# A recurrent attention layer and two feed-forward layers on one core: a new hand-written order for the first 1100 steps

## The chip, the cores and the metric

The kernel runs on one core of a Trainium2 chip. The metric is the device time of one execution in microseconds (us), from runs on the chip. The profile and the trace are of one execution, whose span runs from the first to the last instruction of the core.

## What is computed

Three layers follow one another. The first is a gated recurrent attention with 4 batches, 8 heads, 768 positions and a head dimension of 40. The second and third are feed-forward layers on 3072 tokens of 320 features with 2048 hidden features, both in float32.

```python
for t in range(S):
    m_new = np.maximum(f_gate[:, :, t] + m, i_gate[:, :, t])
    f_stab = np.exp(f_gate[:, :, t] + m - m_new)
    i_stab = np.exp(i_gate[:, :, t] - m_new)
    C = f_stab * C + i_stab * outer(vt, kt)
    n = f_stab * n + i_stab * kt
    y[:, :, t] = sigmoid(o_gate) * (C @ qt) / np.maximum(np.abs(n @ qt), 1.0)
x = y as (3072, 320)
h = x @ w_in;  x = (h * np.clip(h + 3, 0, 6) / 6) @ w_out
h = x @ w2_in; x = np.maximum(h, 0) ** 2 @ w2_out
```

## The kernel before

**Attention.** The recurrence is cut into chunks of 64 positions. A unit is one batch and one chunk; there are 48 units, and a unit of a batch needs the state that the unit before it in the same batch left. The first eight units are (batch 0, 1; chunk 0), (batch 0, 1; chunk 1), then the same for batches 2 and 3. For a unit u the steps are: loads (`at_qk`, `at_kn`, `at_va`), decay weights (`at_rg`, L349, and `w_pe`, L371 and L373, and `w_e`, L393, for the first 16 units; `at_gload`, `w_add`, `w_mask`, `w_e` with L380, L386 and L404 later), scores `at_S` (L450 to L465), their product with the weights `at_P` (L474 to L481), weighted keys `x_k` (L422, L425), output and new state `at_Y` (L492), copy of the state `at_C` (L500), and the normalisation `at_n1` (L508 to L512), `at_n2` (L522 on ACT, L525 on DVE), `at_n3` (L535), which multiplies the output gate in tile X by the result. The gates come first: `gate_m`, `gate_g`, `gate_G`, `gate_b`, `gate_bT` (L277 to L324), in part 0 for the first four chunks and part 1 for the rest. `o_sig` (L542) applies the sigmoid to the output gate of two chunks.

**Feed-forward.** Two chunks of all four batches make a token block of 512 columns. `t_pe` (L639) transposes one batch of it on PE, `t_hi` (L652) and `t_lo` (L668, L670) split the result into two tiles xs. A slot s is one block times 128 hidden features: `mm_A` (8 matmuls, L683), `act1` (ACT, L692), `act1b` (DVE, L701), `act2` (the rounded copy gh, ACT or DVE, L709), `act2b` (the rest gl, DVE, L714), and per batch `mm_B` (3 matmuls, L724). The slots 0 to 7 and 8 to 15 hold half a block each, 0 to 7 of batches 0 and 1, and 8 to 15 of batches 2 and 3; from slot 16 on a slot is a whole block. Weights arrive as 64-bit words (`w_load`, L565) and are unpacked by `w_exp` (ACT, L577), `w_b1` and `w_b2` (DVE, L583 and L589), `w_hi` (L598) and `w_lo` (L603, POOL or DVE). Weight 2i is the i-th eighth of w_in and weight 2i+1 that of w_out.

**What sets the order.** Each engine runs its instructions in the order in which the program issues them, and all loads and stores go through one queue, SP's. The table FIRST (L32 to L119) lists steps with their arguments and, behind an @, the engine where it isn't the usual one (a is ACT, v is DVE, g is POOL). All steps of FIRST are issued in that order, and then those of a planned sequence that FIRST doesn't hold:

```python
todo = [(steps[name], *args) for each entry of FIRST]
early = set(todo)
todo += [step for step in seq if step not in early]
for f, *a in todo:
    f(*a)
```

Of the kernel before, what the change touches and what calls it, by code (L numbers as in the profile page):

```python
# [38 lines left out]
at_Y:1 at_rg:4 w_load:0,3 at_C:0@v at_n1:0 w_load:0,10 at_n2:0@a w_load:0,9 w_pe:4 at_rg:5@v
at_kn:4 at_n1:1 at_n3:0@g at_S:2 at_n2:1 at_C:1@v x_k:2 at_va:6 w_hi:0,0 at_n3:1@g w_exp:0,1 w_pe:5  # L40
at_P:2,0 w_e:4 at_rg:6 at_S:3 w_load:0,4 at_qk:5 w_lo:0,0@v w_exp:0,7 w_b1:0,1 at_Y:2 w_e:5
w_b2:0,1 w_exp:0,2 at_qk:6 at_P:3,0 x_k:3 w_pe:6 w_hi:0,1 at_n1:2 at_rg:7 at_n2:2@a at_S:4
w_load:0,8 w_b1:0,2 w_b2:0,2 at_C:2 w_pe:7 w_exp:0,3 at_rg:8@v at_kn:5 at_P:4,0 at_n3:2@g w_hi:0,2
at_Y:3 w_e:7 w_lo:0,2 w_e:6 t_pe:0,0,0 at_n1:3 at_kn:6 w_exp:0,9 at_C:3@v w_load:0,6 t_hi:0,0,0
at_n2:3@a at_va:7 at_n3:3 t_lo:0,0,0 x_k:4 t_pe:0,0,1 w_lo:0,1 w_exp:0,10 at_Y:4 t_hi:0,0,1@v
at_va:8 t_lo:0,0,1 w_exp:0,4 at_va:9 w_b1:0,3 at_qk:7 mm_A:0 at_C:4 w_b1:0,4 at_n1:4 w_b2:0,4
mm_A:1 act1:0 at_kn:7 at_n2:4 w_hi:0,4 at_va:10 act1b:0 at_S:5 at_n3:4@g act2:0@v at_qk:8 act1:1
act2b:0 w_exp:0,8 w_lo:0,4 act1b:1 mm_A:2 at_P:5,0 act2:1 mm_B:0,1 act2b:1 act1:2 w_load:0,11
at_S:6 w_exp:0,6 w_b2:0,3 at_qk:9 mm_A:3 x_k:5@v w_hi:0,3 act1b:2 x_k:6 at_kn:8 at_Y:5 at_P:6,0
act2:2 w_load:0,5 w_lo:0,3 act1:3 mm_B:0,0 at_va:11 act2b:2 at_C:5 at_S:7 act1b:3 at_va:12 at_n1:5  # L50
act2:3 at_n2:5 x_k:7 at_qk:10 mm_A:4 at_P:7,0 at_kn:9 at_Y:6 w_exp:0,11 w_b1:0,6 load_gates:1
w_b2:0,6 w_pe:8 act1:4 mm_B:1,0 at_C:6 mm_B:2,0 act2b:3 at_rg:9 w_e:8 mm_B:1,1 act1b:4 w_hi:0,6
mm_B:2,1 at_n1:6 w_pe:9 at_rg:10 at_n2:6 act2:4 mm_B:3,1 w_exp:0,5 act2b:4 mm_B:3,0 at_n3:6 w_e:9
mm_A:5 w_b1:0,5 w_lo:0,6@v at_Y:7 act1:5 o_load:3 w_b2:0,5 at_S:8 x_k:8@a at_qk:11 at_n1:7 mm_A:6
at_P:8,0 o_load:2 at_C:7 act1b:5 w_pe:10 at_rg:11 w_hi:0,5 w_load:0,13 w_b1:0,8 o_load:1 at_n3:5
act2:5 act1:6 w_load:0,12 act2b:5 w_lo:0,5 w_e:10 act1b:6 mm_A:7 at_va:13 act2:6@v o_sig:3
w_load:0,14 at_n2:7@a t_pe:0,0,2 act2b:6 at_n3:7@g at_kn:10 mm_B:4,1 t_hi:0,0,2@v mm_B:5,1 at_kn:11
t_lo:0,0,2 mm_B:4,0 mm_B:5,0 w_b1:0,7 t_pe:0,0,3 w_b2:0,7 at_va:14 gate_m:1 act1:7 at_Y:8 w_hi:0,7
act1b:7 at_va:15 t_hi:0,0,3 w_lo:0,7 at_n1:8 act2:7 at_n2:8@a t_lo:0,0,3 act2b:7 mm_A:8 gate_g:1
at_va:16 o_sig:1 mm_B:6,1 mm_B:7,1 at_C:8 act1:8 mm_A:9 w_b2:0,8 gate_G:1 w_exp:0,13 w_exp:0,12  # L60
mm_B:6,0 w_hi:0,8 mm_B:7,0 act1b:8 at_n3:8@g at_S:9 act1:9 act2:8@v act2b:8 o_sig:2 w_lo:0,8
act1b:9 mm_A:10 at_qk:12 act2:9@v w_exp:0,14 act2b:9 mm_B:8,2 at_P:9,0 mm_B:8,3 act1:10 mm_A:11
w_b1:0,12 act1b:10 mm_B:9,2 w_b1:0,9 act2:10 w_pe:11 act1:11 act2b:10 at_rg:12 mm_B:9,3 act1b:11
w_e:11 mm_A:12 gate_b:1 mm_B:10,2 mm_B:10,3 act2:11 x_k:9@v at_kn:12 at_S:10 act1:12 w_b2:0,12
o_load:5 at_Y:9 act2b:11 x_k:10 w_hi:0,12 at_kn:13 at_P:10,0 mm_A:13 at_C:9 w_lo:0,12 act1b:12
at_va:17 mm_B:11,3 at_n1:9 act2:12 mm_B:11,2 at_n2:9 at_qk:13 act1:13 at_S:11 act1b:13 at_n3:9@g
act2b:12 act2:13 at_Y:10 act2b:13 at_va:18 w_b2:0,9 mm_A:14 at_C:10 gate_bT:1 w_hi:0,9 at_qk:14
mm_A:15 act1:14 x_k:11@v o_load:4 mm_B:12,2 act1b:14 w_lo:0,9 act1:15 at_kn:14 mm_B:12,3 at_P:11,0
act2:14 mm_B:13,3 mm_B:13,2 act2b:14 w_pe:12 w_b1:0,10 mm_A:16 act1b:15 at_rg:13 w_e:12 at_n1:10
act2:15 at_n2:10@a act2b:15 w_b1:0,14 at_S:12 w_b2:0,14 act1:16 mm_A:17 at_qk:15 w_b2:0,10  # L70
w_hi:0,14 act1b:16 w_lo:0,14 mm_B:14,2 at_P:12,0 act1:17 mm_B:15,2 act2:16@v mm_B:14,3 w_pe:13
act1b:17 at_rg:14 mm_B:15,3 w_e:13 act2b:16 at_Y:11 act2:17 w_hi:0,10@v w_pe:14 at_va:19 at_C:11@v
at_rg:15 mm_B:16,3 w_e:14 mm_B:16,1 at_n1:11 mm_B:16,2 at_n2:11@a w_lo:0,10 act2b:17 w_load:0,15
at_S:13 mm_B:17,3 at_P:13,0 at_qk:16 mm_B:16,0 mm_B:17,0 w_b1:0,11 w_pe:15 w_b2:0,11 mm_A:18 w_e:15
at_n3:11 w_hi:0,11 x_k:12@v w_exp:0,15 x_k:13@v at_gload:16 mm_B:17,2 at_n3:10 at_kn:15 act1:18
at_Y:12 w_b1:0,15 at_va:20 mm_A:19 act1b:18 w_lo:0,11 at_C:12 at_n1:12 at_kn:16 at_n2:12@a
at_gload:17 act2:18@v w_add:16 at_S:14 act2b:18 w_b2:0,15 mm_B:18,3 act1:19 at_qk:17 at_Y:13
w_b1:0,13 w_hi:0,15 mm_A:20 w_b2:0,13 at_va:21 at_C:13 x_k:14@a at_n1:13 w_add:17 at_n2:13 act1b:19
mm_B:17,1 w_mask:16 mm_B:18,1 at_P:14,0 act2:19 mm_B:18,0 at_kn:17 w_mask:17 mm_B:18,2 at_gload:18
w_e:16 act2b:19 at_S:15 act1:20 at_n3:12 at_n3:13 w_hi:0,13 mm_B:19,3 at_qk:18 mm_B:19,0 at_P:15,0  # L80
x_k:15@a w_lo:0,13 mm_B:19,2 act1b:20 at_S:16 at_Y:14 w_lo:0,15@v act2:20 mm_A:21 at_kn:18 at_va:22
at_n1:14 w_add:18 w_e:17 act2b:20 at_gload:19 at_C:14 at_n2:14 w_mask:18 mm_A:22 act1:21 x_q:16
at_P:16,1 at_P:16,0 w_e:18 act1b:21 t_pe:0,1,0 act2:21 x_k:16@v mm_B:20,0 at_qk:19 mm_B:20,2
t_hi:0,1,0@v at_n3:14@g act1:22 at_gload:20 at_Y:15 t_lo:0,1,0 at_va:23 mm_B:20,3 w_add:19 act2b:21
at_C:15 t_pe:0,1,2 mm_B:19,1 at_n1:15 at_kn:19 mm_A:23 w_mask:19 at_n2:15@a act1b:22 x_q:17
act2:22@v t_hi:0,1,2@v mm_B:21,0 w_e:19 t_lo:0,1,2 w_add:20 mm_B:20,1 act1:23 mm_B:21,3 act2b:22
# [829 lines left out]
```

## Time and profile before

| what | us |
|---|---|
| median of 3 runs (826.83 to 830.62) | 827.2 |
| the profiled execution | 827.76 |
| its span | 826.0 |
| PE busy | 801.1 (97%) |
| DVE busy | 541.9 (66%) |
| ACT busy | 424.8 (51%) |
| POOL busy | 226.8 (27%) |

PE is TensorE, DVE is VectorE, ACT is ScalarE, POOL is GpSimd and SP is the engine that issues the transfers. The shares are means over the whole span. On the page's view in 40 slices PE is busy for nine tenths or more in all slices but the first two, the fourth and the last, and its granted clock is below full in the second and, less, in the fourth.

### The profile page before, as it was taken

The numbers are of one execution on the slowest core, as the hardware profiler recorded it, in microseconds if no ns is written. First come the engines' busy times: TensorE is split into PE (matmuls) and PEld (weight loads), VectorE is DVE, ScalarE is ACT, GpSimd is POOL, SyncE is SP. The second block draws the span as 40 slices with busy tenths as digits, with TensorE's granted clock in tenths as the row PEclk, the third lists the DMA queues.
The fourth block names the chain that finished last, engine by engine and source line by source line (L and its number), as shares of the span: only waits on it lengthen the run. The fifth ranks groups of instructions, "written<-read, shape, count | busy, mean of one in ns | idle before, by whom it ended". The sixth has DMA issues, their size and how long they took to land.

```text
span 826.0 us, 19222 instructions
## 1 busy us (share of the span) xinstructions
PE 801.1 (97%) x7896; PEld 712.3 (86%) x7896; DVE 541.9 (66%) x967; ACT 424.8 (51%) x839; POOL 226.8 (27%) x201
## 2 busy tenths in 40 slices
...
GB/s 230 295 187 182 119 124 72 128 92 72 145 103 108 86 148 99 90 148 36 53 55 235 203 172 1 1 71 1 34 37 1 71 2 1 33 1 0 33 2 33
DMA packets 39332, 72.26 MB, mean 87 GB/s; under 512 B 5420, under 2 KB 25452, under 8 KB 39244
## 3 DMA queue, kind: packets, MB, share of 16 engines
...
q14 instruction: 26, 0.21, 0.1%
...
## 4 chain that ended last, share of the span: by engine, by line
PE 91%; ACT 3%; DVE 3%; issue 2%; POOL 1%; ACTq 0%; DVEq 0%; POOLq 0%
PE hps L683 42%; PE acc L724 40%; PE Yp L492 4%; PE Sp L458 2%; PE tp L639 1%; PE Sp L450 1%; DVE qs L436 1%; PE Sp L452 1%; ACT yt L522 1%; PE Sp L465 0%; PE Wp L373 0%; ACT X L542 0%; DVE X L731 0%; ACT L542 0%; ACT g L692 0%
## 5 line engine op out<-in xcount | busy, mean ns | idle before, releaser
L683 PE MATMUL hps<-xs,wi 128*128 128x512 f32 (+1 forms) x1600 | 389.6, 386 | 1.5 <-DVE gl L714 1.0
L724 PE MATMUL acc<-wo,gh 128*128 128x320 f32 x1536 | 346.2, 312 | 0.0
L683 PEld LDWEIGHTS hps<-xs,wi 128*128 128x128 f32 x1600 | 287.5, 190 | 51.4 <-DVE gl L714 1.6
L724 PEld LDWEIGHTS acc<-wo,gh 128*128 128x128 f32 x1536 | 260.9, 188 | 11.8
L724 PE MATMUL acc<-wo,gl 128*128 128x320 f32 x768 | 237.6, 309 | 0.0
L714 DVE TENSOR_TENSOR gl<-g,gh 128x512 fp32r<-128x512 f32 x176 | 130.6, 743 | 63.2 <-ACT gh L709 61.0
L704 DVE TENSOR_TENSOR g<-g 128x512 f32<-128x512 f32 x96 | 66.4, 691 | 124.3 <-ACT g L694 124.3
L724 PEld LDWEIGHTS acc<-wo,gl 128*128 128x128 f32 x768 | 144.4, 188 | 0.2 <-DVE gl L714 0.2
L692 ACT ACTIVATE g<-hps,less 128x512 f32<-128x512 f32 (+1 forms) x104 | 68.1, 656 | 138.2 <-PE hps L683 126.9
L709 ACT CAST gh<-g 128x512 fp32r<-128x512 f32 x169 | 104.4, 619 | 61.8 <-DVE g L704 49.3
L694 ACT ACTIVATE g<-hps 128x512 f32<-128x512 f32 x96 | 57.3, 597 | 144.7 <-PE hps L683 144.7
L701 DVE SCALAR_TENSOR_TENSOR g<-g,hps 128x512 f32<-128x512 f32 x80 | 54.6, 685 | 52.8 <-ACT g L692 52.6
L414 POOL TENSOR_TENSOR Xm<-qkt,W 40x512 f32<-40x512 f32 x31 | 40.8, 1315 | 105.8 <-ACT W L404 81.2
L603 POOL TENSOR_TENSOR wi<-wt,wi 128x768 fp32r<-128x768 f32 x14 | 27.3, 1953 | 106.9 <-ACT wi L598 101.7
L380 POOL TENSOR_TENSOR W<-W,bT 104x512 f32<-104x512 f32 x32 | 44.8, 1401 | 17.5 <-DMA W<-Gd 12.8
L492 PEld LDWEIGHTS Yp<-Z,Xm 104*32 104x32 f32 (+1 forms) x3072 | 34.8, 110 | 14.1 <-issue 10.9
L492 PE MATMUL Yp<-Z,Xm 104*32 104x41 f32 (+1 forms) x3072 | 40.7, 208 | 0.9 <-issue 0.9
L436 DVE SCALAR_TENSOR_TENSOR qs<-qs,less,qkt 120x512 fp32r<-120x512 f32 x52 | 37.9, 769 | 3.3 <-ACT qs L434 3.1
L603 POOL TENSOR_TENSOR wo<-wt,wo 128x640 fp32r<-128x640 f32 x15 | 24.8, 1656 | 27.6 <-ACT wo L598 27.5
L535 DVE TENSOR_TENSOR X<-X,yt 64x320 f32<-64x320 f32 x34 | 30.1, 887 | 3.0 <-ACT yt L522 2.1
L425 POOL TENSOR_TENSOR Xm<-kI,W 104x320 f32<-104x320 f32 x32 | 30.1, 939 | 5.0 <-DVE pre L349 3.1
L450 PEld LDWEIGHTS Sp<-qkt 40*64 40x64 f32 x256 | 19.3, 157 | 13.3 <-issue 6.6
(110 smaller groups left out, 674.4 us busy)
## 6 DMA issues: line engine op xcount, KB each, us to landing
...
```

The lines of the kernel that those rows point to most:

```text
L380: on("w_add", "g", u).tensor_tensor(out=W, in0=W, in1=bT[:, c - NC1, b * H:(b + 1) * H].unsqueeze(2).to_broadcast([KX, H, L]), op=ALU.add)
L436: nc.vector.scalar_tensor_tensor(out=y[0:KS, i], in0=y[0:KS, i].bitcast(F32), scalar=less[0:KS, i:i + 1], in1=x[0:KS, i], op0=ALU.mult, op ...
L492: nc.tensor.matmul(out=Yp[o:e, h, :], lhsT=Xm[:, h, o:e], rhs=Z[b][c % 2][:, h, :], start=True, stop=True)
L603: on("w_lo", "g", ph, i).tensor_tensor(out=w[:, 1], in0=f, in1=w[:, 0].bitcast(F32), op=ALU.subtract)
L683: nc.tensor.matmul(out=h, lhsT=w[:, hl, kk, o:o + P], rhs=t[:, xk, i0 * P:i1 * P], start=(i == 0), stop=(i == len(TERMS) - 1))
L692: nc.scalar.activation(out=g, in_=T["h", s], func=ACTF.Relu, bias=three)
L694: nc.scalar.activation(out=g, in_=T["h", s], func=ACTF.Relu)
L701: nc.vector.scalar_tensor_tensor(out=g, in0=r, scalar=6.0, in1=T["h", s], op0=ALU.min, op1=ALU.mult)
L704: nc.vector.tensor_tensor(out=g, in0=r, in1=r, op=ALU.mult)
L709: copy("act2", s)(out=gh, in_=g)
L714: nc.vector.tensor_tensor(out=gl, in0=g, in1=gh.bitcast(F32), op=ALU.subtract)
L724: nc.tensor.matmul(out=acc[i], lhsT=g[:, n], rhs=w[:, hl, m % MG, :], start=(m == 0 and q == 0), stop=(m == NM - 1 and q == 2))
```

## The change

The table FIRST is replaced: it held 898 steps and now holds 1100. The engine marked behind an @ is the same for every step. The 202 steps that come in were in the planned sequence that follows the table; 32 of them issue no instruction (`x_q` for the first 16 units, and the second half of `at_P` for these and from unit 22 on). The table now reaches to `act2b:48` and `mm_B:46`, where it reached to `act2b:39` and `mm_B:37`. No function is changed; the lines behind the table move down by 19, so L393 here is L412 there.

```diff
 FIRST = """
-const_z:2 const_i load_gates:0 const_z:3 head_rows:3@g const_m head_rows:2 const_l const_o
...
-x_k:26@a at_P:25,0 act2b:39
+x_q:14 const_i const_z:3 const_o load_gates:0 head_rows:2 const_k:2 at_qk:1 const_z:0 at_va:0
+w_load:0,0 const_m x_q:13 head_rows:3@g head_rows:1 const_g gate_m:0 gate_g:0 gate_G:0 at_qk:0
...
+at_n3:29 mm_B:46,3 at_P:7,1 at_P:24,1 mm_B:46,2
 """
```

Three places show what moves. The first is ACT ahead of slot 0. In the rows W<-Wp is `w_e`, rwi or rwo is `w_exp`, Z<-Yp is `at_C`, yt is `at_n2`, xs is `t_hi:0,0,0`, wi and wo are `w_hi`. Before:

```order
L522 ACTIVATE yt_483<-Yp_432,rd_478 64x40 x8
L500 COPY Z00_101<-Yp_432 40x328
L577 ACTIVATE rwo1_342<-rwo1_342 128x640
L598 CAST wi1_525<-wt_512 128x768
L393 ACTIVATE W_516<-Wp_517 104x512
L393 ACTIVATE W_472<-Wp_473 104x512
L577 ACTIVATE rwo4_360<-rwo4_360 128x640
L652 CAST xs_563<-tp_564 128x3x128
L522 ACTIVATE yt_578<-Yp_527,rd_568 64x40 x8
```

And of the change:

```order
L596 ACTIVATE rwo1_368<-rwo1_368 128x640
L519 COPY Z00_101<-Yp_419 40x328
L541 ACTIVATE yt_520<-Yp_419,rd_455 64x40 x8
L541 ACTIVATE yt_540<-Yp_461,rd_494 64x40 x8
L412 ACTIVATE W_532<-Wp_533 104x512
L671 CAST xs_556<-tp_557 128x3x128
L617 CAST wi1_600<-wt_459 128x768
```

The second yt, `at_n2:3`, now stands directly behind the first, `at_n2:2`, and ahead of the transposed block's copy; seven instructions stood between the two.

The second place is ACT between slots 5 and 8, around the sigmoid `o_sig:3` of tile X3 and `at_n2:7` (the yt row ahead of it or behind it). Before:

```order
L692 ACTIVATE g_1051<-hps_1023,less_96 128x256
L393 ACTIVATE W_1036<-Wp_1037 104x512
L542 ACT_TABLE_LOAD
L542 ACTIVATE X3_112<-X3_112 128x1280
L522 ACTIVATE yt_1075<-Yp_954,rd_1019 64x40 x8
L692 ACTIVATE g_1117<-hps_1060,less_96 128x256
L598 CAST wo3_1152<-wt_1108 128x640
L652 CAST xs_563<-tp_1110 128x3x128
```

And of the change:

```order
L711 ACTIVATE g_1035<-hps_1011,less_96 128x256
L412 ACTIVATE W_1022<-Wp_1023 104x512
L541 ACTIVATE yt_1047<-Yp_937,rd_1026 64x40 x8
L617 CAST wo3_1068<-wt_1032 128x640
L711 ACTIVATE g_1081<-hps_1072,less_96 128x256
L728 CAST gh_1084<-hps_1072 128x256
L671 CAST xs_556<-tp_1131 128x3x128
L519 COPY Z01_102<-Yp_1086 40x328
L561 ACT_TABLE_LOAD
L561 ACTIVATE X3_112<-X3_112 128x1280
```

The table load and the sigmoid went from ahead of `at_n2:7` to behind the last copy of the block, xs of `t_hi:0,0,3`.

The third place is DVE around the scan of the second part of the gates, `gate_m:1` (L277, L296 in the change), and the last split of the first block, `t_lo:0,0,3` (the two rows that write xs from tp). Before:

```order
L589 SCALAR_TENSOR_TENSOR wt_1108<-rwo3_249,wt_1108 128x640
L277 SCALAR_TENSOR_TENSOR X5_114<-X4_113,X5_114 32x512
L701 SCALAR_TENSOR_TENSOR hps_1060<-g_1117,hps_1060 128x256
L508 TENSOR_SCALAR Yp_1119<-Yp_1119 64x8
L511 TENSOR_SCALAR Yp_1119<-Yp_1119 64x8
L512 RECIPROCAL rd_1158<-Yp_1119 64x8
L668 TENSOR_TENSOR xs_563<-tp_1110,xs_563 128x2x128
L670 TENSOR_TENSOR xs_563<-tp_1110,xs_563 64x128
```

And of the change:

```order
L733 TENSOR_TENSOR gl_1125<-hps_1011,gh_1066 128x256
L687 TENSOR_TENSOR xs_556<-tp_1131,xs_556 128x2x128
L689 TENSOR_TENSOR xs_556<-tp_1131,xs_556 64x128
L296 SCALAR_TENSOR_TENSOR X5_114<-X4_113,X5_114 32x512
L608 SCALAR_TENSOR_TENSOR wt_1061<-rwi4_896,wt_1061 128x768
L720 SCALAR_TENSOR_TENSOR hps_1151<-g_1161,hps_1151 128x256
```

The scan stood six instructions ahead of the end of the split and now stands right behind it, ahead of the first activation of slot 8.

## Rows read from the trace of the kernel before

**Rows 1.** Busy time by stage; columns: stretch, length, PE, PEld, DVE, ACT, POOL, clock, DMA.

```profile
0.00:38.56 38.56, 23.96 (x503) 17.13 (x503) 30.37 (x60) 27.54 (x57) 22.91 (x32) 0.78 0.88 269
38.56:68.85 30.29, 26.39 (x501) 23.56 (x497) 25.17 (x53) 21.75 (x49) 15.19 (x11) 0.89 0.74 230
68.85:92.30 23.45, 22.95 (x345) 21.27 (x341) 21.33 (x43) 16.72 (x34) 11.97 (x10) 0.91 0.45 123
92.30:137.90 45.60, 45.60 (x797) 39.20 (x795) 39.45 (x84) 28.57 (x81) 26.24 (x25) 1.00 0.33 95
230.00:826.00 596.00, 591.15 (x4588) 531.54 (x4586) 349.76 (x592) 280.89 (x507) 110.85 (x89) 1.00 0.21 63
```

**Rows 2.** PE's waits over the whole span: total, times, longest.

```profile
PE Sp L450 <- DMA qkt<-in_qk: 5.5, 1, 5.5
PE Sp L450 <- issue: 3.8, 1, 3.8
PE tp L639 <- DVE xs L670: 3.8, 1, 3.8
PE tp L639 <- POOL X L535: 2.9, 1, 2.9
PE Sp L458 <- DVE qs L436: 1.3, 3, 0.8
...
PE hps L683 <- DVE gl L714: 1.0, 1, 1.0
PE Yp L492 <- issue: 0.9, 1, 0.9
PE hps L683 <- DVE xs L668: 0.5, 1, 0.5
```

**Rows 3.** PE in order of time around slots 0 and 8: start, length.

```profile
36.51 0.87 PE L639 MATMUL tp<-ident,X 128*128 128x128 f32 x3 [3.78 <-DVE xs L670]
37.31 1.31 PE L492 MATMUL Yp<-Z,Xm 104*32 104x41 f32 x64
...
66.77 0.90 PE L639 MATMUL tp<-ident,X 128*128 128x128 f32 x3 [2.89 <-POOL X L535]
67.60 1.32 PE L492 MATMUL Yp<-Z,Xm 104*32 104x41 f32 x64
...
69.94 1.44 PE L683 MATMUL hps<-xs,wi 128*128 128x256 f32 x5 [0.51 <-DVE xs L668]
```

**Rows 4.** ACT in order of time ahead of slot 0 and around 62 us.

```profile
31.14 1.08 ACT L393 ACTIVATE W<-Wp 104x512 f32<-104x512 f32 x2
...
33.30 1.55 ACT L522 ACTIVATE yt<-Yp,rd 64x40 f32<-64x40 f32 x8
...
60.95 1.28 ACT L542 ACT_TABLE_LOAD   x1
62.25 1.27 ACT L542 ACTIVATE X<-X 128x1280 f32<-128x1280 f32 x1
63.53 1.55 ACT L522 ACTIVATE yt<-Yp,rd 64x40 f32<-64x40 f32 x8
```

**Rows 5.** DVE in order of time: the end of the first gates, and the wait for yt.

```profile
10.34 0.41 DVE L320 TENSOR_TENSOR pre<-gt,pre 32x256 fp32r<-32x256 f32 x1
...
34.88 0.74 DVE L535 TENSOR_TENSOR X<-X,yt 64x320 f32<-64x320 f32 x1 [2.05 <-ACT yt L522]
```

**Rows 6.** Busy time of single microseconds: the clock after the second wait (columns as in Rows 1).

```profile
66.00:67.00 1.00, 0.23 (x1) 0.23 (x2) 0.48 (x2) 0.20 (x1) 0.92 (x2) 0.58 0.98 403
...
72.00:73.00 1.00, 1.00 (x6) 1.00 (x5) 1.00 (x2) 0.95 (x3) 0.52 (x1) 0.51 0.15 30
73.00:74.00 1.00, 1.00 (x10) 1.00 (x9) 1.00 (x1) 1.00 (x3) 0.58 (x1) 1.00 0.04 5
```

**Rows 7.** Issues of SP in order of time: an output gate's load, and the one that waits for it.

```profile
8.28 0.42 SPq L538 DMA_DIRECT2D X<-in_og  x1
...
15.87 0.47 SPq L341 DMA_DIRECT2D kI<-in_kn  x1
```

More of the change, by code (lines that the diff above doesn't have):

```diff
@@ L39 @@
[L39 to L86, printed above, removed]
```

136 lines of the change are left out of this document (101 added, 35 removed).

## The prediction

> **What bounds the kernel now.** I read the busy time by stage first. I cut the span where slots begin on PE: slot 0 at 38.56 us, slot 8 at 68.85, slot 16 at 92.30, slot 24 at 137.90 [rows 1]. The reader is to see two things. From 68.85 on PE is busy for all but a few us, and for 591.15 of the last 596.00: there the time is PE's work, and an order can't make that smaller. Ahead of 68.85 PE is busy for 23.96 of 38.56 and for 26.39 of 30.29 us, and the granted clock is 0.78 and 0.89. So nearly all that a new order can win lies in the first 70 us. The second thing is DVE in the same rows. It is busy for 25.17 of 30.29 (83%), then for 21.33 of 23.45 (91%) and for 39.45 of 45.60 (87%). A PE that comes earlier finds a DVE with little room.
>
> The second view is PE's waits [rows 2]. The first wait, 5.5 us for the first load, is the start. Three more are long: 3.8 us put down to "issue" (no other engine named), 3.8 us of the transposes for DVE's split (L670), and 2.9 us of the transposes for POOL's product into X (L535). Then come short ones: 1.0 for gl, 0.5 for xs, and, after 200 us, 1.3 and 0.9.
>
> The third view is the order of time around the two waits of the transposes. The first ends at 36.51 [rows 3]. Behind it stands a chain through ACT: two W exponentials begin at 31.14, and only at 33.30 the eight yt activations of unit 3 start [rows 4]; DVE stands 2.05 us waiting for yt, and then, at 34.88, multiplies it into X [rows 5]. DVE's split of the block already transposed is queued behind that product, and PE's second transpose waits for the split. The second wait ends at 66.77 [rows 3]. On ACT a table load of 1.28 us and a sigmoid of 1.27 us stand directly ahead of the yt activations of unit 7 at 63.53 [rows 4], and POOL's product of that unit releases PE. The granted clock then averages 0.58 in the microsecond from 66, is 0.51 in that from 72 and 1.00 in the next [rows 6]: PE works at its lower level (1.2 GHz) for about 6 us behind that wait.
>
> **The change, part by part.** The instructions and their engines stay; the count of table loads stays as well. Each term is against the profiled execution: span 826.0, time 827.76. That is 0.56 above the median of 827.2, so I take the sum of the terms off 827.2.
>
> *To slot 0.* The listing of ACT shows `at_n2:3` directly behind `at_n2:2`; exponentials and weight steps that stood between are behind it or earlier. Of the chain this removes the stretch from 31.14 to 33.30, 2.2 us [rows 4]. DVE no longer waits there, and the split is no longer queued behind it when the second transpose wants its buffer. What is late next is unit 3's product itself: the second transpose needs its rows, so the rest of the 3.8 us stays covered by that chain. The far end of the gain: the issue wait of 3.8 us [rows 2] lies in the scores of unit 2, and if DVE and ACT have other work in that time it costs nothing, 6.0 us together. The far end of the loss: SP now issues the first weight fifth instead of twelfth, ahead of the loads of q and k for unit 0, and ACT has its `w_exp:0,0` ahead of the last head rows, which the gates' last steps need. The nearest row is an output gate's load, the thirteenth issue at 8.28, on which a later issue waited until 15.87 [rows 7], 7.6 us. At 0.64 us an issue (8.28 over 13) the weight is issued at 3.2 and lands at 10.8 by that row; four ACT instructions at the stage's mean of 27.54/57 = 0.48 [rows 1] and DVE's 0.41 end at 13.1 where the gates now end at 10.75 [rows 5]. That is 2.4 late, and 0.2 net. Between a gain of 6.0 and a loss of 0.2 I take **2.2**, the stretch that the order removes by itself; the issue wait isn't set by the table.
>
> *Slot 0 to slot 8.* The table load and the sigmoid, 1.28 + 1.27 = 2.55 us [rows 4], move behind `at_n2:7`. PE's wait of 2.9 shrinks by as much. Without it the clock needn't fall. Work at the lower level in this stage is 66.77 to 68.85, 2.08 us; at the upper it would take about half, so 1.04. Together **3.6**. The load now stands behind the block's last copy, where the next ACT work is slot 7's or 8's activation, and two further slots of `mm_B` cover that. DVE's cover: the listing has two instructions fewer between slots 0 and 8, and 25.17 us less two at 25.17/53 = 0.47 [rows 1] is 24.2 in a stage of 26.7, 91%. Bounds: nothing, if another wait fills the gap, to 4.9, if the rest of the 2.9 and the 1.0 for gl go as well.
>
> The Trainium skill (ScalarE: Activation LUTs, "What ACT_TABLE_LOAD costs") states 1283 ns for the load and about 1380 ns more of draining, some 2.66 us for a switch. The trace has 1.28 for the load and the sigmoid 0.02 us behind its end [rows 4], so it shows no draining, and I take the row. By the page the whole wait of 2.9 would go, and the sum would be 0.3 lower.
>
> *Slot 8 to slot 16.* The wait of 0.5 for xs goes [rows 2], and 69.94 to 73.0 at the lower clock [rows 3, 6], 3.06 us, halves: together a gain of 2.0, and PE's stage would be 21.4. Against it stands DVE. The listing has six DVE instructions more between the two slots (`gate_m:1`, steps of units 10 and 12, a weight's `w_b2`, `act1b:15`). At 21.33/43 = 0.50 each [rows 1] that is 3.0 us, and DVE's work 24.3, which is 2.9 above PE's. At the present share of 91% it would be 26.7, a loss of 5.3; if PE needs none of the added steps in time, 0. I take **2.9**, between the two: the steps stand ahead of slot 16's own activation in one queue. Net of the stage: a loss of 0.9.
>
> *Slot 16 on.* From 92.30 to 137.90 PE is busy throughout [rows 1], so there is nothing to win. DVE has seven instructions more up to slot 20, but nine fewer up to slot 24. After that the table replaces an order with 2.2 us of waits (1.3 and 0.9) [rows 2]; I take no change, with 2.2 either way. Behind slot 48 the sequence is what it was.
>
> Sum: 2.2 + 3.6 - 0.9 = 4.9 us. The span goes to 821.1, the profiled execution to 822.9, the median to **822.3**.
>
> **The rivals.**
>
> *DVE keeps up.* The issue wait is covered too (6.0), the second wait goes (3.6), the clock stays up (2.0), and DVE's added steps cost nothing. 11.6 us, so 815.6. For it: DVE idles 8.2 us of its first 38.56, more than it would need to give. Against it: 91% later. Chance 0.20.
>
> *Given back.* Slot 0 comes no earlier, since another load or the issue wait takes the chain's place, and DVE runs at its share of 91% from slot 8: 3.6 + 2.0 - 5.3 = 0.3 gained, 826.9. For it: PE is full and DVE nearly so in every stage after slot 8 [rows 1]. Chance 0.22.
>
> *DVE paces, and the clock falls (slower).* Place: slots 8 to 20. If DVE's added work comes in front of what PE waits for, PE loses 5.3 up to slot 16 and seven instructions at 39.45/84 = 0.47, 3.3, up to slot 20: 8.6 us. In gaps of 2.9 as at 63.9 that makes three, and each is followed by work at the lower clock at the price found above, 1.04 + 1.53 = 2.6. Together 16.4, less the 7.8 saved ahead of it: 8.6 slower, 835.8. It decides where the gaps grow from a few tenths, as now, to the 2.9 behind which the clock fell. Against it: the granted clock is 1.00 from 92.30 on, whatever short waits there are [rows 1]. Chance 0.11.
>
> That the order isn't what the table says is no rival: the listing shows each moved row.
>
> **How the numbers follow.** The forecast's own case has 0.47, and gives 818 to 826 by its bounds; two thirds of it lie below 823.1. A measurement of this kernel tells about 0.5%, 4.1 us, from no change. Faster by more: 0.31 of the forecast's case, 0.20 of the first rival, 0.01 of the second: 0.52. Within: 0.16, 0.20 of the second: 0.36. Slower: the third and a rest of the second, 0.12. The range reaches from 814, below the first rival by its uncertain later waits, to 831, which leaves out most of the third rival and a rest of the first.
>
> **What would show it.** Slot 0's first matmul (L702 there) near 36.4 us; no long wait of the transposes for POOL's X ahead of slot 8, which starts near 63; a table load behind the block's last copy; a granted clock of 1.00 from the fourth slot to the sixteenth. DVE's share between slots 8 and 16 at or above 95%, with PE's waits there naming DVE, together near 2.9. The forecast is wrong if slot 0 starts later than 38.6, if a new wait over 2 us stands after slot 8, or if the issue wait grows or goes.

## The result, and the profile after

The changed order takes **835.5 us** (median of 6 runs, 834.71 to 839.18), the order before 827.19 (826.83 to 830.62). The ratio is 1.01, with a 95% interval from 1.0077 to 1.0124. The forecast was 822.3, with a range of 814 to 831. The profiled execution of the changed kernel took 834.71, and its span is 832.9 us, 6.9 above the 826.0 of before.

The page of the changed kernel: span, busy time of each engine, and the chain that ended last by engine and by line (lines are 19 higher than before: L702 is the first product of a slot, L743 the second, L469 the scores, L511 the outputs of an attention unit).

```profile
span 832.9 us, 19206 instructions
...
PE 804.3 (97%) x7896; PEld 713.7 (86%) x7896; DVE 533.2 (64%) x967; ACT 425.0 (51%) x839; POOL 220.8 (27%) x201
...
PE 81%; DMA 6%; DVE 6%; ACT 4%; issue 1%; SPq 1%; POOL 1%; ACTq 0%; POOLq 0%; DVEq 0%
```

The same work is done, and the chain is still PE's for 81%. PE's idle time grew from 24.9 (826.0 less 801.1 busy) to 28.6 us. Busy time by stage of the changed kernel, cut where its slots 0, 8, 16 and 24 start, with a last row behind them; the columns are those of [rows 1].

```profile
0.00:37.60 37.60, 23.22 (x502) 17.40 (x502) 26.55 (x60) 25.55 (x54) 17.99 (x26) 0.85 0.80 238
37.60:71.76 34.16, 29.34 (x504) 26.64 (x504) 24.14 (x58) 20.86 (x51) 16.25 (x19) 0.81 0.54 164
71.76:94.67 22.91, 21.87 (x366) 19.58 (x365) 20.84 (x38) 18.73 (x37) 10.37 (x11) 1.00 0.58 177
94.67:141.34 46.67, 45.27 (x765) 38.13 (x764) 38.94 (x82) 28.85 (x82) 25.01 (x23) 1.00 0.39 107
141.34:205.00 63.66, 61.60 (x747) 52.03 (x746) 48.20 (x93) 32.37 (x74) 27.35 (x26) 1.00 0.41 110
```

Against [rows 1] slot 0 starts 0.96 us earlier, but the stage from slot 0 to slot 8 takes 34.16 instead of 30.29 at a clock of 0.81 instead of 0.89. DVE is busy for 20.84 of 22.91 us between slots 8 and 16, 91%, as before. And in the last two rows PE is no longer busy throughout, as it was from 92.30 to 137.90.

Such a stage holds a little more or less of the attention's work in one order than in the other. So I compare at slots ahead of which PE has done **the same work** in both. PE's order is known from the table, and a step's length from where PE is full (0.96 us for a first product below slot 16 and 1.84 from it, 0.44 for a second, 1.08 or 0.45 for scores, 0.73 for outputs, 0.45 for a transpose, 0.46 for W). The sums are equal ahead of slot 0 (13.6), 10 (40.9), 14 (52.3) and 39 (156.8). PE in order of time, the first products of these slots, the changed kernel:

```profile
37.60 0.58 PE L702 MATMUL hps<-xs,wi 128*128 128x256 f32 x1
...
76.27 0.39 PE L702 MATMUL hps<-xs,wi 128*128 128x256 f32 x1 [0.29 <-DVE gl L733]
...
89.60 0.39 PE L702 MATMUL hps<-xs,wi 128*128 128x256 f32 x1
...
204.43 0.48 PE L702 MATMUL hps<-xs,wi 128*128 128x512 f32 x1
```

The same view of the kernel before, slots 10, 14 and 39 (slot 0 starts at 38.56):

```profile
76.11 0.39 PE L683 MATMUL hps<-xs,wi 128*128 128x256 f32 x1
...
88.05 0.39 PE L683 MATMUL hps<-xs,wi 128*128 128x256 f32 x1
...
196.80 0.39 PE L683 MATMUL hps<-xs,wi 128*128 128x512 f32 x1
```

So the 6.9 us are: -0.96 to slot 0, +1.12 from slot 0 to 10, +1.39 from 10 to 14, +6.08 from 14 to 39, and -0.73 from there to the end. Two places lose. Neither is a chance of this one profile: four of the kernels below that keep the changed order from slot 0 to 9 (e6, e10, e11, e13) take 38.45 to 39.46 us from slot 0 to 10, two with the order before (e5, e12) 36.49 and 37.89; and four that keep the changed order from slot 14 on (e1, e2, e5, e6) take 114.5 to 115.4 from there to slot 39.

**The first is at 51 to 67 us.** The waits of the changed kernel from 46 to 62 us (engine and operation, what ended the wait, total, times, longest):

```profile
POOL wo L622 <- ACT wo L617: 9.2, 1, 9.2
ACT rwi L596 <- DMA rwi<-in_w1i: 5.2, 1, 5.2
DVE gl L733 <- ACT gh L728: 4.8, 2, 4.0
...
PE Sp L469 <- ACT W L412: 3.0, 1, 3.0
...
PE Yp L511 <- issue: 1.8, 1, 1.8
```

ACT in order of time there, and SP's issues ahead of it:

```profile
51.47 0.60 ACT L412 ACTIVATE W<-Wp 104x512 f32<-104x512 f32 x1
57.32 0.88 ACT L596 ACTIVATE rwi<-rwi 128x768 f32<-128x768 f32 x1 [5.25 <-DMA rwi<-in_w1i]
```

```profile
35.61 1.40 SPq L584 DMA_DIRECT2D rwi<-in_w1i  x1
44.07 0.47 SPq L360 DMA_DIRECT2D kI<-in_kn  x1
...
47.83 0.50 SPq L584 DMA_DIRECT2D rwi<-in_w1i  x1
```

`w_exp:0,8` stands in ACT's queue at slot 5, for a weight of slot 16. Its load `w_load:0,8` (768 KB) was issued at 47.83, since SP stood at `at_kn:8` from 37.0 to 44.07, and landed at 57.3. ACT waits for it 5.25 us, with gh of slot 4, g of slot 5 and the next W queued behind it; DVE waits for gh, POOL for the weight's half, and PE, after an issue wait of 1.82 us, 3.00 for W. Busy time of short stretches: behind these waits the clock is at its lower level (1.2 GHz).

```profile
54.00:56.00 2.00, 0.39 (x40) 0.27 (x29) 0.46 (x1) 0.00 (x0) 0.00 (x0) 1.00 1.00 275
56.00:58.00 2.00, 0.88 (x7) 0.55 (x6) 0.00 (x0) 0.68 (x1) 0.00 (x0) 0.81 1.12 278
58.00:60.00 2.00, 0.00 (x0) 0.00 (x0) 1.34 (x3) 2.00 (x6) 0.00 (x0) 0.50 1.05 346
60.00:66.00 6.00, 5.90 (x47) 5.51 (x48) 4.31 (x11) 4.56 (x17) 1.55 (x1) 0.50 0.19 66
```

**The second is spread from slot 10 to slot 39.** There are many short waits. They are seen best on PE's weight loads (PEld); the waits of the changed kernel from 76.27 to 204.4:

```profile
PEld Yp L511 <- issue: 2.4, 10, 0.6
PEld acc L743 <- DVE gl L733: 1.5, 5, 0.4
PEld hps L702 <- DVE g L720: 1.4, 2, 1.1
PEld Sp L469 <- ACT rwo L596: 1.1, 1, 1.1
```

The kernel before, 76.11 to 196.8:

```profile
PEld Yp L492 <- issue: 1.6, 7, 0.4
PEld Sp L450 <- issue: 1.3, 5, 0.4
PEld Sp L465 <- issue: 0.9, 4, 0.4
```

Over all rows of these two views, 18 waits that end with another engine's work sum to 8.2 us, against 8 with 1.8 before, and those put down to issue to 4.7 against 3.8. The difference, 7.3, is about the 7.47 us that this stretch lost.

### The profile page after: what moved, and what is told of

The parts are those of the page before. It is cut to its first block, busy times and chain, and to the rows that moved or that the text cites. A ratio compares the mean times of both kernels' runs of the same rounds, so it can differ in the third digit from the quotient of the medians.

```text
span 832.9 us, 19206 instructions
## 1 busy us (share of the span) xinstructions
PE 804.3 (97%) x7896; PEld 713.7 (86%) x7896; DVE 533.2 (64%) x967; ACT 425.0 (51%) x839; POOL 220.8 (27%) x201
## 3 DMA queue, kind: packets, MB, share of 16 engines
q8 instruction: 62, 1.02, 0.5%
## 4 chain that ended last, share of the span: by engine, by line
PE 81%; DMA 6%; DVE 6%; ACT 4%; issue 1%; SPq 1%; POOL 1%; ACTq 0%; POOLq 0%; DVEq 0%
PE hps L702 39%; PE acc L743 36%; PE Yp L511 2%; DMA rwi<-in_w1i 2%; PE Sp L477 2%; DMA W<-Gd 1%; DMA kI<-in_kn 1%; DMA rwo<-in_w1o 1%; ACT g L711 1%; PE tp L658 1%; DMA qkt<-in_qk 1%; DVE gl L733 1%; ACT Xm L441 1%; DVE g L720 1%; DVE qs L455 0%
## 5 line engine op out<-in xcount | busy, mean ns | idle before, releaser
L702 PE MATMUL hps<-xs,wi 128*128 128x512 f32 (+1 forms) x1600 | 389.9, 386 | 1.2 <-DVE g L720 0.9
L743 PE MATMUL acc<-wo,gh 128*128 128x320 f32 x1536 | 347.0, 313 | 0.1
L702 PEld LDWEIGHTS hps<-xs,wi 128*128 128x128 f32 x1600 | 286.6, 189 | 51.4 <-DVE g L720 1.4
L743 PEld LDWEIGHTS acc<-wo,gh 128*128 128x128 f32 x1536 | 261.3, 189 | 13.2 <-ACT gh L728 0.4
L743 PE MATMUL acc<-wo,gl 128*128 128x320 f32 x768 | 238.5, 310 | 0.5 <-DVE gl L733 0.3
L733 DVE TENSOR_TENSOR gl<-g,gh 128x512 fp32r<-128x512 f32 x176 | 127.7, 726 | 65.3 <-ACT gh L728 63.1
L743 PEld LDWEIGHTS acc<-wo,gl 128*128 128x128 f32 x768 | 144.6, 188 | 2.0 <-DVE gl L733 2.0
L713 ACT ACTIVATE g<-hps 128x512 f32<-128x512 f32 x96 | 57.3, 597 | 144.7 <-PE hps L702 144.7
L511 PEld LDWEIGHTS Yp<-Z,Xm 104*32 104x32 f32 (+1 forms) x3072 | 34.7, 109 | 15.7 <-issue 13.2
L399 POOL TENSOR_TENSOR W<-W,bT 104x512 f32<-104x512 f32 x32 | 41.8, 1307 | 23.4 <-DMA W<-Gd 23.1
L511 PE MATMUL Yp<-Z,Xm 104*32 104x41 f32 (+1 forms) x3072 | 40.7, 208 | 2.1 <-issue 1.8
L469 PE MATMUL Sp<-qkt 40*64 40x64 f32 x256 | 23.0, 253 | 13.8 <-DMA qkt<-in_qk 9.4
L469 PEld LDWEIGHTS Sp<-qkt 40*64 40x64 f32 x256 | 20.4, 164 | 17.4 <-DMA qkt<-in_qk 9.4
```

What stands on the lines that cost most here:

```text
L399: on("w_add", "g", u).tensor_tensor(out=W, in0=W, in1=bT[:, c - NC1, b * H:(b + 1) * H].unsqueeze(2).to_broadcast([KX, H, L]), op=ALU.add)
L469: nc.tensor.matmul(out=Sp[0:L, h, :], lhsT=qkt[E0:KX, 1, h, :], rhs=q, start=True, stop=True)
L511: nc.tensor.matmul(out=Yp[o:e, h, :], lhsT=Xm[:, h, o:e], rhs=Z[b][c % 2][:, h, :], start=True, stop=True)
L702: nc.tensor.matmul(out=h, lhsT=w[:, hl, kk, o:o + P], rhs=t[:, xk, i0 * P:i1 * P], start=(i == 0), stop=(i == len(TERMS) - 1))
L713: nc.scalar.activation(out=g, in_=T["h", s], func=ACTF.Relu)
L733: nc.vector.tensor_tensor(out=gl, in0=g, in1=gh.bitcast(F32), op=ALU.subtract)
```

## The experiments

Each edit is in the one table; the lines below show the pieces of it. In all kernels the starts of slots 0, 10, 14 and 39 are read as above, from one profile each; times are medians, the interval is that of the ratio to the order before, which ran beside each kernel (its medians lie between 826.49 and 827.99). The granted clock between 24 and 48 us is 1.00 in some profiles (e1, e6, e7, e9, e11) and 0.50 in a large part of that stretch in others (e2, e10, e13, e14), so the start of slot 10 carries that too; from slot 14 to 39 kernels with the same order agree within 1 us.

| kernel | time | interval | slot 0 | slot 10 | slot 14 | slot 39 | 14 to 39 |
|---|---|---|---|---|---|---|---|
| before | 827.19 | | 38.56 | 76.11 | 88.05 | 196.80 | 108.75 |
| changed | 835.5 | 1.0077-1.0124 | 37.60 | 76.27 | 89.60 | 204.43 | 114.83 |
| e1 | 832.79 | 1.0042-1.0084 | 39.03 | 74.69 | 88.03 | 202.97 | 114.94 |
| e2 | 831.09 | 1.0031-1.0069 | 38.38 | 72.30 | 85.62 | 200.90 | 115.28 |
| e3 | 827.30 | 1.0002-1.0021 | 38.10 | 74.31 | 87.55 | 196.28 | 108.73 |
| e4 | 842.34 | 1.015-1.022 | 39.43 | 79.44 | 100.52 | 209.26 | 108.74 |
| e5 | 835.20 | 1.0068-1.0111 | 39.81 | 76.30 | 89.99 | 204.47 | 114.48 |
| e6 | 836.01 | 1.0075-1.0114 | 38.91 | 77.81 | 91.15 | 206.53 | 115.38 |
| e7 | 830.02 | 1.0023-1.0061 | 38.59 | 70.34 | 83.69 | 198.22 | 114.53 |
| e8 | 825.18 | 0.9956-0.9979 | 38.07 | 71.97 | 85.53 | 194.28 | 108.75 |
| e9 | 830.31 | 1.0013-1.0044 | 38.20 | 74.04 | 87.39 | 199.51 | 112.12 |
| e10 | 838.65 | 1.0089-1.0146 | 39.95 | 79.41 | 93.33 | 210.85 | 117.52 |
| e11 | 846.5 | 1.0206-1.0245 | 40.22 | 79.07 | 96.67 | 217.78 | 121.11 |
| e12 | 833.68 | 1.0053-1.0086 | 38.39 | 76.28 | 88.24 | 202.05 | 113.81 |
| e13 | 835.47 | 1.0057-1.0097 | 40.05 | 78.50 | 91.83 | 206.25 | 114.42 |
| e14 | 830.91 | 1.0018-1.006 | 39.52 | 78.04 | 91.41 | 205.15 | 113.74 |
| e15 | 840.82 | 1.0148-1.0198 | 39.49 | 73.28 | 87.51 | 209.49 | 121.98 |
| e16 | 838.06 | 1.0122-1.0156 | 37.90 | 71.78 | 85.11 | 206.14 | 121.03 |

**The held weight: e1 and e2.**

```diff
 mm_B:2,0 w_load:0,8
-w_exp:0,8
 at_va:10
...
 mm_B:4,1 w_e:10
+w_exp:0,8
 mm_B:3,0
```

> The changed order with one ACT step moved: w_exp:0,8 (the 0.6 us expansion of a weight for slot 16) stands 47 steps later, behind w_e:10, its load stays where it is. Theory A (ACT's in-order queue is held by a weight that nobody needs yet: 5.25 us of waiting for the transfer, and gh, W and g of slots 4 to 6 behind it): the 7.0 us that the change loses between PE works at 53.6 and 63.9 mostly go, time 829 to 831, the idle PE of 3.0 us before the attention unit 8 is gone. Theory B (the transfers of 44 to 57 us are bunched, and the next one to be late takes the place of this wait): PE stands for another load, time 834 to 836.

832.79: 2.7 us better, half of what theory A said. (The expansion takes 0.88 us in the row above, not 0.6.) PE's wait of 3.0 for W is gone, but the issue wait stayed (1.64 us), and the clock averages 0.58 from 60 to 66 us all the same. PE, and the clock right behind:

```profile
57.30 0.25 PE L500 MATMUL Yp<-Z,Xm 104*32 104x41 f32 x4 [1.64 <-issue]
```

```profile
58.00:60.00 2.00, 2.00 (x35) 1.76 (x33) 1.27 (x2) 0.88 (x4) 0.12 (x1) 0.55 1.12 267
```

```diff
 w_load:0,6 w_exp:0,6
+w_load:0,8
 at_kn:8
...
 mm_B:2,0
-w_load:0,8
 w_exp:0,8
```

> The changed order with one SP step moved: the load of that weight, w_load:0,8 (768 KB), goes ahead of at_kn:8, at which SP stands from 37.0 to 44.1 us, and w_exp:0,8 stays in its place. Theory A: the load is then issued near 37 us and landed by 50, ACT's wait of 5.25 us is gone, time 829 to 831 as in the run with the later expansion. Theory B: 768 KB go ahead of the k and v loads of units 8 to 10, these come up to 3 us later and attention waits for them, time 834 to 837. If only the place on ACT mattered and not the load's issue, nothing changes: 835.

831.09, near theory A's 829 to 831; theory B is out. Slot 0 to slot 10 takes 33.92 us instead of 38.67. Busy time of the kernel with the early load: neither the wait nor the fall of the clock is there.

```profile
54.00:56.00 2.00, 2.00 (x15) 1.84 (x15) 1.97 (x4) 1.99 (x5) 0.37 (x1) 1.00 1.04 178
56.00:58.00 2.00, 2.00 (x77) 1.57 (x77) 1.97 (x5) 2.00 (x4) 0.00 (x0) 1.00 1.11 298
```

Either end of this wait, pulled by itself, ends it, and ACT waits for no load there in either kernel. Which is the better to pull the times don't tell, as the two intervals overlap; what e1 keeps is the issue wait and the clock behind it. Behind slot 14 nothing changed in either kernel.

**The sigmoid alone: e3 and e8.**

```diff
 at_va:13 act2:6@v
-o_sig:3
 w_load:0,14 at_n2:7@a
...
 act2b:7 mm_A:8
+o_sig:3
 gate_g:1 at_va:16
```

> The order before with one step moved: o_sig:3 (table load 1.28 us and sigmoid 1.27 us on ACT) goes from ahead of at_n2:7 to behind mm_A:8, as the changed order has it, and all else stays. Theory C (these two stood in the chain to slot 8, as the prediction says for slots 0 to 8): time 822 to 824. By the comparison of both traces at equal PE work, where the change wins back 6.0 us between its slots 7 and 9: down to 821. Rival D (another work on ACT, or POOL's add of the block, ends the same wait a little earlier, and the table load now stands in the chain to slot 9): 826 to 828.

827.30, no gain: rival D. PE's wait of 2.9 us for X [rows 2] is gone, and a new one of 2.54 stands in the first product of slot 10. PE and ACT of this kernel in order of time (mm_A is on L674 here):

```profile
74.31 0.86 PE L674 MATMUL hps<-xs,wi 128*128 128x256 f32 x5 [2.54 <-DVE gl L705]
```

```profile
68.20 1.28 ACT L533 ACT_TABLE_LOAD   x1
69.50 2.43 ACT L533 ACTIVATE X<-X 128x1280 f32<-128x1280 f32 x2
71.95 0.43 ACT L491 COPY Z<-Yp 40x328 f32<-40x328 f32 x1
72.41 0.47 ACT L683 ACTIVATE g<-hps,less 128x256 f32<-128x256 f32 x1
```

Now the table load, two sigmoids and a copy, 4.2 us in one piece, stand ahead of slot 8's activation, DVE gets its input at 72.9, and slot 10 needs the buffer that DVE frees. Slot 10 starts 1.8 us earlier than before, slot 14 only 0.5.

e8 spreads this work out, so that no slot's activation has more than one sigmoid ahead of it:

```diff
 gate_m:1 act1:7
+o_sig:3
 at_Y:8 w_hi:0,7
...
-mm_A:8 gate_g:1 at_va:16 o_sig:1 mm_B:6,1 mm_B:7,1 at_C:8 act1:8 mm_A:9
+mm_A:8 act1:8 gate_g:1 at_va:16 o_sig:1 mm_B:6,1 mm_B:7,1 at_C:8 mm_A:9
+act1b:8 act2:8@v act2b:8
 w_b2:0,8
...
 act1:10
+o_sig:2
 mm_A:11
...
 act1:11
+w_exp:0,13 w_exp:0,14
```

> The order before with ACT's work of slots 7 to 11 spread out: o_sig:3 with its table load behind act1:7, act1:8 straight behind mm_A:8, o_sig:1 behind it, o_sig:2 behind act1:10, two weight expansions behind act1:11, DVE's three steps of slot 8 ahead of the gates' and the weight's work. Theory D (the 4.4 us that the later sigmoid alone won at slot 9 were given back because ACT then did 7 us of table load, two sigmoids, a copy and expansions in one piece ahead of slots 8 and 9): 822.5 to 824.5. Rival I (DVE, 96% busy from 62 to 70 us there, sets the pace to slot 12, so whatever ACT gives is taken by DVE): 826 to 828.

825.18, faster than the order before by 0.2 to 0.4%, just outside theory D's range: slot 10 starts 4.1 us earlier than before, and 2.5 are left at slot 14 and at slot 39. ACT of this kernel in order of time:

```profile
62.32 0.48 ACT L692 ACTIVATE g<-hps,less 128x256 f32<-128x256 f32 x1
62.81 1.28 ACT L542 ACT_TABLE_LOAD   x1
64.11 1.27 ACT L542 ACTIVATE X<-X 128x1280 f32<-128x1280 f32 x1
...
68.34 0.47 ACT L692 ACTIVATE g<-hps,less 128x256 f32<-128x256 f32 x1
68.72 1.26 ACT L542 ACTIVATE X<-X 128x1280 f32<-128x1280 f32 x1
```

It is the only kernel here that beats both orders.

**The start: e6.**

```diff
+at_qk:0
 w_load:0,0 const_m x_q:13
...
-at_qk:0
-w_exp:0,0
 gate_b:0 at_kn:0 head_rows:0
+w_exp:0,0
```

> The changed order with its start as before in two steps: at_qk:0 is issued ahead of w_load:0,0, and w_exp:0,0 stands behind head_rows:0 on ACT. The first matmul comes at 5.5 us instead of 9.4 in each theory. Theory G (the start of the change loses its 1.2 us against the forecast because the first weight's 768 KB go ahead of q and k of the first units): 833 to 834.5. Rival H (the gate chain and the weight's own conversion set slot 0, and the early matmuls only wait elsewhere): 835 to 836, and slot 0 within 0.5 us of 37.6.

836.01, rival H in the time: the first product came at 7.2 us (not 5.5, as each theory said) and slot 0 at 38.91, later than in the profile of the changed kernel and inside what the same start gives anyway: in the twelve kernels with the changed start, slot 0 begins between 37.60 and 40.22, 39.0 on the mean; in the five with the start before between 38.07 and 39.81, 38.6 on the mean.

**Where the second loss belongs: e4, e5, e7, e9.**

```diff
 at_n2:8@a act1b:8 at_S:9
-mm_A:9 act1:9 x_k:9@v w_exp:0,12 act2:8@v
+w_load:0,9 w_exp:0,9 at_va:9 at_va:11 at_va:12
...
+gate_g:1 mm_A:9 gate_G:1 w_exp:0,13 w_exp:0,12
...
```

> The changed order up to mm_A:9 (about 74 us), then the steps left over in the order before. Theory E (the second loss of the change, some 8 us between slots 9 and 38, belongs to the new order of those slots: a dozen waits of 0.3 to 1 us): the loss of the head stays and is 0 at slot 9, that of the rest goes, time 826 to 829. Rival F (the rest is slow because the head leaves less work done ahead, so any order meets it): 832 to 836.

842.34, above both theories, but the place is plain. ACT meets expansions whose loads were issued just ahead of them, and waits 5.46 us for one:

```profile
84.84 0.76 ACT L569 ACTIVATE rwo<-rwo 128x640 f32<-128x640 f32 x1 [5.46 <-DMA rwo<-in_w1o]
```

Behind the join, slot 14 to 39 takes 108.74 us, as before (108.75). e5 is the counterpart, without such expansions at its join:

```diff
 mm_B:7,1 at_C:8 act1:8
-mm_A:9 w_b2:0,8 gate_G:1 w_exp:0,13
+w_b2:0,8 at_rg:12 act1b:8 at_S:9 mm_A:9 act1:9
...
```

> The order before up to mm_A:9 (about 73 us), then the steps left over in the changed order; 18 steps, weight loads among them, are done earlier than the changed order had them, 8 small ones later. Theory E (the second loss belongs to the changed order of slots 9 to 38): the head of before, and on it the 8 us by which the changed order falls behind before between equal PE works at slots 9 and 38: 833 to 836. Rival F (the second loss is what the head of the change left behind): 826 to 829.

835.20, theory E. From slot 10 to 39 it takes 128.17 us, the changed kernel 128.16, the order before 120.69. So the head, the order up to the join (the place where one order passes into the other), has no part in the second loss.

```diff
 w_mask:16 at_va:14 w_hi:0,11 w_lo:0,11 at_kn:14
-mm_A:19 act1b:18 at_n2:12@a at_S:14
+o_load:4 at_va:19 mm_B:16,3 mm_B:17,3 at_qk:16 w_exp:0,15 w_b1:0,15 at_va:20 mm_A:19
...
```

> The changed order with w_load:0,8 issued early (as in the run before with that load alone, 831.1) up to mm_A:19 (about 105 us), then the steps left over in the order before. Theory E: between PE works of slots 19 and 38 the changed order lost 9.1 us and the order before 3.9, so 5.2 us come back: 825 to 827. Rival F: 830 to 832.

830.02, rival F's number without its mechanism: the join costs again (the weight's load, issued at 96.28, was waited for until 105.39, and DVE's conversions stood behind it). Slot 19 starts 4.2 us earlier than before (103.94 against 108.17), slot 21 1.4 later (121.82 against 120.40); from slot 21 on the order before is as fast as ever (76.40 us to slot 39 in both). e9 moves that weight's steps back:

```diff
-w_exp:0,15 w_b1:0,15
 at_va:20 mm_A:19
...
 x_k:14@a
+w_exp:0,15
 at_n1:13
...
 act1b:19
+w_b1:0,15 w_b2:0,15
```

> As the run with the early w_load:0,8 and the order before from mm_A:19 on (830.0), but the expansion and the three conversions of weight 0,15, which stood right at the join and whose load came 9 us after its issue, are 10 to 40 steps later. If that join alone cost the 6.2 us that were lost there at equal PE work, the time is 823 to 825, below both orders. If the order before needs that weight early, or the head's gain is given back elsewhere, 827 to 830.

830.31, not the 823 to 825: the same head, which reached slot 10 at 70.34 in e7, got there at 74.04, and the join still cost some.

**What in the order of slots 10 to 39 does it: e10 to e13.**

```diff
 gate_G:1
+mm_B:10,3
 mm_A:11 act1:11
...
 act2:30@v
+mm_B:28,1 mm_B:29,0
 mm_A:31
```

> The changed order with PE's order alone changed after slot 9: at eight of the dozen places where PE waited 0.3 to 1 us, one or two products mm_B (0.44 us each, 13 in all), whose operands are ready, are taken from later and put ahead of the step that waited. Theory J (PE takes a step too soon after the DVE or ACT work that feeds it, and ready work stood behind it): 3 to 5 us of these waits go, 830.5 to 832.5. Rival K (DVE, about 84% busy there and in order, sets the pace, so a wait that is filled comes back at a later step): under 1 us, 834.5 to 836.

838.65: theory J falls, and the time is above rival K's too. With ready products pulled ahead of the waiting step, slots 14 to 39 take 117.5 us in the profile (841.10, the slowest of its four runs), 2.7 more. Its waits there are 1.65 us put down to issue, 1.00 of the first products for g and 0.65 of the outputs for yt; ahead of slot 14 the second products wait 1.14 for gh. That this order is worse than the changed one is not shown, as the intervals overlap; that it is no better is.

```diff
 mm_A:9
+at_qk:11 at_va:9 at_qk:10 at_kn:10 at_va:11 at_va:15
+at_kn:11 at_va:13 at_qk:12 at_va:12 at_va:14
 act1:9 x_k:9@v
...
```

> The changed order with SP's order alone changed behind mm_A:9: the 56 loads of attention units 9 to 25 (q and k, k by rows, v, gate rows) are issued as far ahead of their first user as the order before issues them, where the reader of the buffer's last content allows it. Measured as PE work between a load's issue step and its user, the mean lead of q and k goes from 7.6 to 13.7 us (16.0 in the order before), of k by rows from 10.9 to 14.6 (17.2), of v from 28.5 to 41.2. Theory L (slots 10 to 39 take 128 us instead of 121 because the changed order issues these loads so late that SP's queue and their landing end the chain): most of the 7.5 us come back, 829 to 831.5, and slot 10 to slot 39 takes 121 to 123.5 us. Rival M (the order of DVE's and ACT's own work sets it, and the loads only came last by a little): under 2 us, 833.5 to 836, and 126 to 128.5 us.

846.5, inconclusive: SP's queue stood at loads whose buffers were still in use (18 us in four waits for scores between 74 and 130 us), with weights behind them, and ACT waited for those. The converse:

```diff
 mm_B:21,1
-at_gload:21
 mm_B:22,1
...
 mm_A:24
+at_va:21 at_kn:19 at_va:24 at_gload:21
 evac:23,1
```

> The reverse: the order before with SP's order alone changed behind mm_A:9, 46 of the same loads issued as late as the changed order issues them (mean lead of q and k 15.1 to 8.8 us of PE work, of k by rows 17.1 to 9.9, of v 54 to 38). Theory L: slots 10 to 39 grow from 120.7 to 125 to 128 us, time 831 to 835. Rival M: within 1.5 us, 826.5 to 829.

833.68, as theory L says in size. But nearly all of the loss lies in one place: one late load of gate rows, unit 21's, holds POOL ahead of the keys of unit 18, and PE waits 3.09 us, then works at the lower clock (eight products in about 2.5 us each time instead of 2.0). It is the first loss over again, on another engine: a step that nobody needs yet waits at the head of a queue.

```profile
146.88 0.79 PE L492 MATMUL Yp<-Z,Xm 104*32 104x41 f32 x60 [3.09 <-POOL Xm L425]
...
149.01 5.12 PE L683 MATMUL hps<-xs,wi 128*128 128x512 f32 x16
```

That isn't the pattern of the changed order's short waits. There, however, SP does stand at a load that isn't due; SP of the changed kernel in order of time:

```profile
87.38 0.35 SPq L584 DMA_DIRECT2D rwi<-in_w1i  x1
96.57 0.47 SPq L360 DMA_DIRECT2D kI<-in_kn  x1
...
101.08 0.47 SPq L360 DMA_DIRECT2D kI<-in_kn  x1
```

From 87.7 to 96.57 it stands at `at_kn:15`, with `at_kn:13` (101.08) behind it. So e13 lets the loads trade places:

```diff
 w_exp:0,14 x_k:12@v
-at_kn:15
+at_kn:13
 at_n3:8@g
...
 w_hi:0,11 w_lo:0,11
-at_kn:14
+at_kn:15
 mm_A:19
```

> The changed order, where only the loads behind mm_A:9 trade places: those of q and k, of k by rows and of v stand in SP's same places, but in the order of the attention units (in the changed order k by rows of unit 15 is issued ahead of 13 and 14 and stands 9.1 us for its buffer, 22 ahead of 21 and 20, and so on; 44 of 68 loads trade). Theory L (SP stands at a load that nobody needs yet, and the needed ones behind it end the chain): slots 10 to 39 take 121.5 to 125 us instead of 128.2, time 829 to 833. Rival M (the order of DVE's and ACT's work sets it): 127 to 128.7 us, time 834 to 836.5.

835.47, and 127.75 us from slot 10 to 39: rival M, not theory L. The order of the loads among themselves isn't the cause. That they come late against their users (e12) is not ruled out by it.

**Together: e14, e15, e16.** e14 has the sorting from slot 0 on and e2's edit; e15 and e16 join the head with e2's edit to the order before, at mm_A:9 and mm_A:14, as e4's piece shows, but with the steps of weights 8 to 14 left at the changed order's slots.

> The same sorting from slot 0 on, and w_load:0,8 ahead of at_kn:8 as in the run with that load alone (831.1). Theories A and L: the gains add, 824 to 829, the order before reached or beaten. Rival M: 830 to 832, as the early load alone.

830.91: the early load's gain alone. Its profile (835.02, among the slowest of its ten runs) doesn't show that gain: ACT waits for no load there, but the clock is at 0.50 from 39.52 to 54 us, and slot 10 starts at 78.04.

> The changed order with w_load:0,8 early up to mm_A:9, then the order before, but the steps of weights 8 to 14 (load, expansion, words, halves) stay at the slots where the changed order has them. Independent terms: slot 10 at 70 to 74 us as in the runs with the early load, and from slot 14 on 108.8 us to slot 39 as in the order before: 820 to 824. Given back: a wait at slots 10 to 14 in the place of those won, 826 to 830.

840.82. The later join:

> The same with the join at mm_A:14, so that slots 10 to 14 run in the changed order and take its 13.3 us instead of 11.9. Independent terms: 821.5 to 825.5, and 108.8 us from slot 14 to slot 39 but for the join. Given back: 827 to 831.

838.06. Both reach slot 10 early (73.28 and 71.78), and both lose 12 to 13 us between slots 14 and 39: PE waits for DVE's gl up to 3.0 us, and ACT 5.2 and 3.9 us for a weight's load. The steps that the changed head had put off fall due among those that the order before does there. Stretches of two good orders don't add up to a third.

## Why the prediction was wrong

*To slot 0, gain 2.2.* The profile of the changed kernel shows 0.96, over all kernels it is a loss of 0.4. The stretch of ACT work did go, and the transposes' wait shrank from 3.8 to 2.2 us. What was mis-sized is what came in its place: the scores wait 9.4 us for their first load instead of 5.5, and an issue wait of 2.8 us (3.8 before) remained. PE's long waits ahead of slot 0 sum to 14.4 us, before to 14.2. Which of them sets slot 0 isn't shown: e6 brought the first load to 7.2, and slot 0 came no earlier. That waits would take each other's place here was the rival "given back".

*Slot 0 to slot 8, gain 3.6.* **This step failed.** The stage took 34.16 us instead of 30.29 (0.88 of that is more of PE's work by the lengths above). Its bound "nothing, if another wait fills the gap" was still too good: even to slot 10, where the work is equal, the changed kernel needs 1.12 us more. Another wait did fill the gap, ACT's 5.25 us for a load, and it was longer than what went. With the load issued early (e2), slot 0 to 10 takes 33.92 us instead of the 37.55 of before, a gain of 3.63. That this is the forecast's 3.6 is luck: with the same order up to slot 10, e7 takes 31.75 and e9 35.84. I had covered the moved sigmoid by what stands behind it, but had not gone through ACT's queue ahead of it for a step that waits for a load. `w_exp:0,8` stood there, its load one place ahead of it in the list, and behind SP's stand at `at_kn:8`. The order showed that; the trace of before showed a load that was waited for until 7.6 us after its issue [rows 7]. And e3 shows that the move alone gains nothing in the order before, because ACT's work was all due in the same 4 us: there two slots of `mm_B` didn't "cover that". In the changed kernel, where one sigmoid and not two stands ahead of slot 8's activation, they did: PE waits 0.29 us at slot 10.

The Trainium skill (ScalarE: Activation LUTs, "What ACT_TABLE_LOAD costs") has about 1380 ns of draining with a table load. ACT of the changed kernel again shows 1.28 us and the sigmoid 0.01 us behind it, so the measurement decides, as in [rows 4]:

```profile
71.43 1.28 ACT L561 ACT_TABLE_LOAD   x1
72.72 1.27 ACT L561 ACTIVATE X<-X 128x1280 f32<-128x1280 f32 x1
```

*Slot 8 to slot 16, loss 0.9.* The stage itself is 0.54 us shorter, as the clock stayed at 1.00, as forecast; that gain lies ahead of slot 10. From slot 10 to 14 the loss is 1.39. DVE's work of 24.3 us, which the term rests on, isn't in the stage: the rows have 38 instructions and 20.84 us, 43 and 21.33 before, and five more than before in the longer stage ahead of it. DVE's share stayed at 91%, below the 95% that I had named as the sign of this step, and the longest wait of PE from slot 10 to 14, 0.7 us, is for ACT's W. DVE is busy from slot 10 to 14 for 11.96 of 13.33 us, before for 10.99 of 11.94, so whether DVE set that loss is not shown.

*Slot 16 on, 0.* **This step failed too**, by 5.4 us (6.08 from slot 14 to 39, less 0.73 to the end). "So there is nothing to win", I wrote, and took it for "nothing to lose". A stretch without waits is the result of an order, and it is the order that was replaced. e5 shows the loss with another head, e4, e3 and e8 show its absence with the order before. Which engine's order in that stretch it is, remains open: PE's products pulled ahead (e10) made it no better, the loads' order (e13) made 0.4 us, the loads' lateness wasn't settled (e11, e12), and DVE's and ACT's own order wasn't exchanged alone.

The third rival's time, 835.8, was met, but not its mechanism: no gap of 2.9 us stands after slot 8, and the clock is 1.00 there. The sum by the steps: forecast -2.2, -2.7 and 0; measured -0.96, +2.51 (slot 0 to 14) and +5.35.
